# Attention rows in runs of 40, a new order of loads and weight turns between forward and GLU, and du placed ahead on VectorE

## The chip, the cores and the metric

The kernel runs on one core of one Trainium2 chip, as one launch. The metric is device time in microseconds (us); the kernel before has a median of 3124.64 us in three runs. The engines are called PE (TensorE, the matmuls), DVE (VectorE), ACT (ScalarE), POOL (GpSimd) and SP (SyncE, which here only issues DMAs); POOL and ACT issue DMAs too.

## The reference

The kernel computes a block with attention over segments and a gated linear unit (GLU), and the gradients of all eleven differentiable inputs. Cut to the forward function, for S = 2048 rows, D = 512, 32 heads of 128, F = 1792:

```python
mod = silu(c) @ w_mod                      # six rows: sa, ca, ga, sb, cb, gb
h = layernorm(x) * (1 + ca) + sa
# attention, segment after segment: 8 memory rows + 32 rows of h
for s in range(64):
    hs = concat([mem, h[32*s:32*s+32]])    # 40 rows
    q, k, v = hs @ Wq, hs @ Wk, hs @ Wv    # 32 heads
    o = softmax(mask(q @ k.T * scale)) @ v
    o = o @ Wo
    mem, a[32*s:32*s+32] = o[:8], o[8:]
x = x + ga * a
h = layernorm(x) * (1 + cb) + sb
out = x + gb * ((sigmoid(h @ w_gate) * (h @ w_up)) @ w_down)
# and the vector-Jacobian product of all this with grad_out
```

The memory rows of a segment come from the segment before, so forward attention is one chain of 64 steps.

## The kernel before, in words

Inputs, weights and most tiles are bf16, sums are f32 in PSUM. There are three stages, one after the other:

- Forward attention (to about 1000 us): a loop over the 64 segments. Four weights, Wq, Wk, Wv and Wo, lie in SBUF. Each segment's probabilities, values and outputs are stored to DRAM for the backward pass (PS, VT, OT, OSR: 352 KB each). Of a segment's 40 output rows, the 8 memory rows are needed at once and the rest only in the GLU. The 8 memory rows and the first 24 of the others are worked out and stored at once (32 rows of AOA, `store_rows` after `tail.split()`); the last 8 rows of four segments are worked out together as a "tail" (`TailRows`) and stored as 32 rows of AOB. Names in PE's records: `ao_tps` are the tail's products, `ao_b_tp` its last turn.
- GLU, forward and backward together (1000 to about 1380 us): 16 tiles of 128 rows go through a software pipeline of seven steps, s0 to s6, in iterations; within one iteration the deepest step (the oldest tile) comes first. w_gate, w_up, w_down lie over the SBUF of Wv and Wk, their turned copies w_gateT and w_upT over Wq.
- Then the weight gradients of the GLU (w_down's chunks, `gps`/`mm` at L1164), and backward attention, of some 1700 us, which the change doesn't touch but for its setup (`WoT`, L1313).

The steps of the GLU, with the names that the records show:

- s0 (L985): `t0` = attention rows x ga, `x1` = t0 + x0, statistics (`st`, `mv`, `ve` on DVE, `rstd` and `db` = dout x gb on POOL), `xhf`, `h2a`, `h2` on DVE. In the records t0 is `t`, x1 is `x`, h2 is `h`.
- s1 (L1021): two transposing DMAs on SP, `hdT<-h` and `hdT<-db`.
- s2 (L1027): four chunks of 448 columns; gate matmuls (L1039), sigmoid on ACT to `sg`, up matmuls (L1043), copy on ACT to `u`; then `hh` = sg x u on DVE, and `umh` = u - hh on POOL.
- s3: `dp` matmuls (hdT of db by w_downT); `du` = dp x sg on DVE in four pieces (L1064), reading PSUM and so freeing the PSUM buffers which later matmuls need; `dg` = du x umh on DVE (L1065).
- s4: `b` = hh by w_down (14 matmuls); transposing DMAs duT and dgT; `b_bf` on ACT; then t1 = b x gb on DVE (L1084, `t`), `o_sb` = t1 + x1 on POOL (L1086) with the store of the output, and `pr_gb` = dout x b on DVE (L1089).
- s5: the gradient of h (28 matmuls); `dh2b` on ACT, `dxh`, `pr_cb`, `junk`, `ta`, `dx` on DVE, `tb` on ACT; `da` = dx x ga on DVE (L1127), `pr_ga` = dx x attention rows on POOL (L1130).
- s6: column sums on PE (`acc_ps`), the turn of da and its store (DAOT).

PSUM has five buffers for the matmuls (psM) and two for the turns (psT).

What sets the order: a scheduler may move instructions of an engine at build time, except where the code pins what is traced between two points (`self.pin`, `pin_behind`). In the kernel before, SP and PE are not among the engines pinned at the end of the GLU, and their order at the seam is the scheduler's: SP issues dout of the first tiles and all the loads of attention rows before the transposing DMAs. The DMAs of one queue use eight completion semaphores in turn, on SP and on POOL, so that each issue waits until the DMA of eight issues before has landed. POOL issues its DMAs (stores, and the GLU's weights at L810) in line with its arithmetic.

At the seam, before: the last segment issues the modulation rows (`mod_bc`, four loads of one row, broadcast over the partitions, into `bcs[2..5]`) and the loads of tile 0 on SP; on POOL the weights in the order w_down, w_up, w_gate; then the late K and Q rows of the last segment (`late_rows`); the turns of the last probabilities (ET, L725) and values (Vst), the end of the tail, and `bcs[4]` + 1. The turns of w_down (L969) come with s0 of tile 0, those of w_up and w_gate (L958) with s0 of tiles 1 and 2; because PE's order is the scheduler's, all those of w_down and w_up were placed before tile 0's first matmul, and evacuated by DVE and ACT in turn.

The loads of attention rows of a tile before are eight DMAs, in `load_x_rows`:

```python
for s4 in range(4):
    q.dma_start(dst[s4 * T:s4 * T + 24, :], a[4 * j + s4, M:32, :])
    q.dma_start(dst[s4 * T + 24:(s4 + 1) * T, :], b[j, 8 * s4:8 * s4 + 8, :])
```

At the end of the GLU, `accs` (a tile of the pool) takes acc_ps and goes to DMOD by four DMAs on POOL; its pool memory is reused by the stage after.

Of the kernel before, what the change touches and what calls it, by code (L numbers as in the profile page):

```python
# [40 lines left out]
class K:  # L41
# [43 lines left out]
    def alloc_dram(self):  # L85
# [6 lines left out]
        self.AOA = d("AOA", [NS + 1, 32, cfg.D], BF16)  # L92
        self.AOB = d("AOB", [NS // 4, 32, cfg.D], BF16)
# [231 lines left out]
    def store_rows(self, psp, pool, ft, dram, name, tag, then=None):  # L325

        nc = self.nc
        tb = pool.tile([128, 128], BF16, name=name + "_tb", bufs=1 if name.endswith("_b") else 2)
        nc.vector.tensor_copy(tb[:].rearrange("p (r c) -> p c r", c=self.cfg.DC), ft[:])

        def f():
            tp = psp.tile([128, 128], BF16, name=name + "_tp", tag=tag)
            nc.tensor.transpose(tp[:], tb[:], self.ident[:])
            rb = pool.tile([128, 128], BF16, name=name + "_rb")
            nc.vector.tensor_copy(rb[:], tp[:])
            nc.gpsimd.dma_start(dram.rearrange("r (c x) -> (r c) x", x=128), rb[:])
            if then is not None:
                then(rb)

        self.later.append(f)  # L340
# [91 lines left out]
    def phase2(self):  # L432
# [13 lines left out]
        with ExitStack() as ctx:  # L446
# [201 lines left out]
            tail = TailRows(self, sb2, psp, psp, 1, "ao", self.AOB, 2, ptag="p")  # L648
# [24 lines left out]
            for s in range(NS):  # L673
# [119 lines left out]
                if s == NS - 1:  # L793
                    for i in range(2, 6):
                        self.mod_bc(None, i, "", t=self.bcs[i])
                    self.glu_first = self.glu_load(0, nc.sync)
# [12 lines left out]
                else:  # L809
                    nc.gpsimd.dma_start(self.w_down, io["B_w_down"].rearrange("(fc p) d -> p fc d", p=128))  # L810
                    nc.gpsimd.dma_start(self.w_up, io["B_w_up"].rearrange("(c p) f -> p c f", p=128))
                    nc.gpsimd.dma_start(self.w_gate, io["B_w_gate"].rearrange("(c p) f -> p c f", p=128))
                    late_rows()
# [56 lines left out]
                self.store_rows(psp, sb2, ft, self.AOA[s + 1], "at", "p")  # L870
# [9 lines left out]
                if s < NS - 1:  # L880
                    norms.append(norm)
            for pi in range(NP):
# [9 lines left out]
            tail.finish()  # L892
# [19 lines left out]
    def glu_load(self, j, q):  # L912
        io, D = self.io, self.cfg.D
        r0, r1 = j * 128, (j + 1) * 128
        x0, a_rows, dout = self.ring_x0[j % 2], self.ring_a[j % 6], self.ring_dout[j % 7]
        q.dma_start(dout, io["grad_out"].rearrange("o s d -> (o s) d")[r0:r1, :])
        self.load_x_rows(a_rows, j, self.AOA[1:], self.AOB, q)
        q.dma_start(x0, io["A_x"].rearrange("o s d -> (o s) d")[r0:r1, :])
        return dict(x0=x0, a_rows=a_rows, dout=dout)

    def phase3(self):
# [9 lines left out]
        with ExitStack() as ctx:  # L931
# [19 lines left out]
            def wT_piece(src, dst, fc0, n, k):  # L951
                def f():
                    for fc in range(fc0, fc0 + n, 2):
# [6 lines left out]
                        self.evac("act" if (fc // 2 + k) % 2 else "dve", dst[:, fc:fc + m, :],  # L960
# [3 lines left out]
            def wdT_piece(c):  # L964
                def f():
                    for f0 in range(0, FC, 7):
# [7 lines left out]
            pieces = {0: [wdT_piece(c) for c in range(DC)],  # L974
                      1: [wT_piece(w_up, w_upT, 0, 8, 0), wT_piece(w_up, w_upT, 8, 6, 0)],
                      2: [wT_piece(w_gate, w_gateT, 0, 8, 1), wT_piece(w_gate, w_gateT, 8, 6, 1)]}
# [3 lines left out]
            def load(j):  # L980
                if j >= NT or j in ins:
                    return
                ins[j] = self.glu_first if j == 0 else self.glu_load(j, nc.sync)

            def s0(j):  # L985
                r0, r1 = j * 128, (j + 1) * 128
                load(j + 1)
                for f in pieces.pop(j, []):
                    f()
# [60 lines left out]

            def s3(j, st):
# [6 lines left out]
                for ch in range(NCH):  # L1058
# [5 lines left out]
                    nc.vector.tensor_tensor(du[:, sl], dp[:, 0:CH], sg[:, sl], op=ALU.mult)  # L1064
                nc.vector.tensor_tensor(dg[:], du[:], umh[:], op=ALU.mult)  # L1065
# [5 lines left out]
            def s4(j, st):  # L1071
# [11 lines left out]
                t1 = sbp.tile([128, D], F32, name="t1", tag="f32tmp", bufs=5)  # L1083
                nc.vector.tensor_tensor(t1[:], b_bf[:], gb_bc[:], op=ALU.mult)  # L1084
                o_sb = sbp.tile([128, D], BF16, name="o_sb", bufs=2)
                nc.gpsimd.tensor_tensor(o_sb[:], t1[:], st["x1"][:], op=ALU.add)  # L1086
                nc.gpsimd.dma_start(out_rows[r0:r1, :], o_sb[:])
                pr = sbp.tile([128, D], BF16, name="pr_gb", bufs=3)
                nc.vector.tensor_tensor(pr[:], st["dout"][:], b_bf[:], op=ALU.mult)  # L1089
                st.update(duT=duT, dgT=dgT, pr=pr)  # L1090
                return st

            def s5(j, st):
# [7 lines left out]
                xh2, rstd, dout, a_rows = st["xh2"], st["rstd"], st["dout"], st["a_rows"]  # L1101
                dh2b = sbp.tile([128, D], BF16, name="dh2b", bufs=1)
# [24 lines left out]
                nc.vector.tensor_tensor(da[:], dx1[:], ga_bc[:], op=ALU.mult)  # L1127
                nc.gpsimd.dma_start(self.DAROWS[r0:r1, :], da[:])
                pr3 = sbp.tile([128, D], BF16, name="pr_ga", bufs=1)
                nc.gpsimd.tensor_tensor(pr3[:], dx1[:], a_rows[:], op=ALU.mult)  # L1130
                st.update(dh2b=dh2b, pr2=pr2, pr3=pr3, da=da)
# [38 lines left out]
            def after(it):  # L1170
                if it == NT + 1:
# [7 lines left out]

            self.run_pipeline(NT, [s0, s1, s2, s3, s4, s5, s6], deepest_first=True, after=after)  # L1180
            ET = mybir.EngineType
            self.pin_behind(i0, self.pinned, [ET.DVE, ET.Activation, ET.Pool])
            accs = sbp.tile([128, D], F32, name="accs", bufs=1)
# [758 lines left out]
class TailRows:  # L1942
# [45 lines left out]
    def split(self):  # L1988
# [5 lines left out]
        def summed():  # L1994
            ft = self.k.fold_sum(self.psp, parts, self.name + "_b", "p")
            self.k.store_rows(self.psp, self.pool, ft, self.dram_b[s0 // 4], self.name + "_b", "p")
# [96 lines left out]
```

The softmax here doesn't subtract the row's maximum and nothing guards it: scores larger than these inputs give would overflow.

## Time and profile before

| quantity | us |
|---|---|
| median of three runs | 3124.64 (3122.74 to 3125.85) |
| the profiled execution | 3127.18 |
| its span | 3125.4 |
| last attention product of forward on PE | 996.1 |
| first gate matmul of tile 0 | 1036.43 |
| start of the second tile's third step and on: steady tiles | 1083 to 1302 |
| last column sums of the GLU | 1379.5 |

The profiled execution is 1.78 us longer than its span: the span runs from the first to the last record of an engine. "Busy" of an engine is the time in which one of its instructions runs. A line of the timeline gives start, duration, engine, line of the code, operation with output and inputs, and, in brackets, the idle time of that engine just before and what ended it. The granted clock of PE is given as a share of full speed. Means by stage, in the GLU's steady tiles: PE 18.91 us busy of 20.13 or 19.70, DVE 15.56 or 15.13, POOL 12.17 or 12.30, ACT 7.25.

### The profile page before, as it was taken

The page shows a single profiled execution, that of the slowest core. Times are in us where ns is not written, and L with a number is a line of the kernel's source. Part 1 is how long each engine was busy: PE and PEld are TensorE (multiplying, and loading weights), DVE is VectorE, ACT ScalarE, POOL GpSimd, SP SyncE. Part 2 cuts the span into 40 slices and gives each one's busy share as a digit, 9 for nine tenths or more (in the row PEclk, how much of TensorE's full clock was granted, in tenths as well). Part 3 has the DMA queues.
Part 4 walks back from the last instruction along what each step waited for, and adds up shares of the span by engine and source line. Part 5 has one row for each costly group of instructions (what it writes and reads, how often), then busy time and mean ns, then how long its engine had stood idle before and what let it go on. Part 6 is the DMA issues. An engine that isn't in the chain of part 4 may idle for free.

```text
span 3125.4 us, 106126 instructions
## 1 busy us (share of the span) xinstructions
PE 3004.2 (96%) x43769; PEld 1838.1 (59%) x43845; DVE 1616.2 (52%) x3738; ACT 1264.6 (40%) x3053; POOL 1473.0 (47%) x2974
## 2 busy tenths in 40 slices
PE   5999999999998799989989999999999999999999
PEld 3666666666665444445567777777777754455454
DVE  4556656655654777733255555555655542322321
ACT  2555555555554433322155555555555530110111
POOL 3666666666665466531144444444444432233322
PEclk8999999999999899999999999999999999999999
DMA  8887788788787798898589999999999998666674
GB/s 295 214 214 199 205 214 212 204 207 213 205 207 237 177 214 219 202 267 271 185 218 244 240 248 242 244 243 248 244 239 244 243 270 285 201 202 213 196 234 147
DMA packets 844665, 703.54 MB, mean 225 GB/s; under 512 B 543794, under 2 KB 716370, under 8 KB 843796
## 3 DMA queue, kind: packets, MB, share of 16 engines
q1 hardware_dynamic: 714404, 486.69, 62.2%
q0 software_dynamic: 59120, 148.64, 14.6%
q10 hardware_dynamic: 70656, 61.41, 6.3%
q8 instruction: 345, 5.65, 0.8%
q14 instruction: 140, 1.15, 0.1%
HBM read 294.93 MB, written 276.35 MB: 183 GB/s over the span
## 4 chain that ended last, share of the span: by engine, by line
PE 50%; issue 4%; DMA 2%; POOL 1%; DVE 0%; SPq 0%; ACT 0%; POOLq 0%; DVEq 0%
PE gps L1885 10%; PE dh_ps L216 8%; PE g_ps L1547 6%; PE pass_ps L256 5%; PE gps5o L1899 4%; PE dhq_ps L224 4%; PE gps L1234 3%; PE dh_tps L216 3%; PE dp_ps L1526 2%; PE tps L1459 2%; PE dp_ps L1534 1%; PE turn_ps L1413 1%; PE dh_ft L321 1%; PE gps L1164 1%; PE wtp L1300 1%
## 5 line engine op out<-in xcount | busy, mean ns | idle before, releaser
L1885 PE MATMUL gps<-rows,hrows 128*128 128x512 bf16 (+2 forms) x2124 | 415.6, 355 | 1.9
L1885 PEld LDWEIGHTS <-hrows 128*128 128x128 bf16 x2160 | 211.2, 98 | 204.6
L256 PEld LDWEIGHTS <-hT 128*32 128x32 bf16 x6144 | 158.2, 97 | 161.3 <-issue 1.9
L1591 POOL COPY dOst<-RAd 96x512 bf16<-96x512 bf16 x128 | 75.4, 613 | 311.3 <-DVE RAd L63 311.1
L1889 POOL DMA_DIRECT2D out_dram<-ot x108 | 81.4, 754 | 258.6 <-DVE ot L63 132.3
L63 DVE CAST ot<-gps 128x512 bf16<-128x512 f32 (+3 forms) x76 | 48.1, 633 | 284.9 <-PE gps L1885 191.6
L875 POOL TENSOR_TENSOR Pst<-Pst,rden 120x1408 bf16<-120x1408 bf16 x63 | 159.6, 2533 | 57.4 <-issue 38.9
L61 ACT ACTIVATE ot<-gps 128x512 bf16<-128x512 f32 (+3 forms) x75 | 41.3, 551 | 356.2 <-PE gps L1885 225.3
L61 ACT ACTIVATE dVT<-g_ps 128x512 bf16<-128x512 f32 (+1 forms) x192 | 109.3, 569 | 95.9 <-PE g_ps L1547 95.5
L63 DVE CAST RA0v<-pass_ps 128x512 bf16<-128x512 f32 x128 | 88.5, 692 | 89.5 <-PE pass_ps L256 86.2
L216 PE MATMUL dh_ps<-WvT,dVT 128*32 128x512 bf16 x2048 | 133.4, 380 | 0.0
L256 PE MATMUL pass_ps<-Wv,hT 128*32 128x512 bf16 x2048 | 133.3, 380 | 0.0
L1899 PE MATMUL gps5o<-WoT,rows 128*128 128x512 bf16 x580 | 127.8, 379 | 1.0 <-DMA rows<-OSR 0.3
L224 PE MATMUL at_ps<-Wo,OT 128*32 128x256 bf16 x4096 | 125.0, 275 | 0.1
L256 PE MATMUL pass_ps<-Wk,hT 128*32 128x512 bf16 x2048 | 123.3, 383 | 1.5 <-ACT hT L865 1.1
L1536 DVE SCALAR_TENSOR_TENSOR dS<-dp_ps,Pst_l 128x512 bf16<-128x512 f32 (+1 forms) x192 | 112.0, 639 | 22.8 <-PE dp_ps L1534 22.8
L256 PE MATMUL pass_ps<-WoT,dyT 128*32 128x256 bf16 (+1 forms) x3072 | 122.4, 308 | 0.9 <-ACT dyT L1665 0.9
L224 PE MATMUL dhq_ps<-WqT,dQT 128*32 128x256 bf16 x4096 | 122.9, 273 | 0.0
L216 PE MATMUL dh_ps<-WkT,dKT 128*32 128x512 bf16 x2048 | 122.3, 380 | 0.0
L256 PE MATMUL pass_ps<-Wq,hT 128*32 128x512 bf16 x2048 | 121.6, 379 | 0.0
L224 PEld LDWEIGHTS <-dQT 128*32 128x32 bf16 x4096 | 109.6, 97 | 15.9
L709 ACT ACTIVATE ET<-st_ps 128x480 bf16<-128x480 f32 (+1 forms) x192 | 96.1, 535 | 42.6 <-ACT qT L61 34.7
(419 smaller groups left out, 7164.5 us busy)
## 6 DMA issues: line engine op xcount, KB each, us to landing
OSR<-Ost SPq DMA_DIRECT2D x64, 352.0 KB
OT<-OT SPq DMA_DIRECT2D x64, 352.0 KB
VT<-VTr SPq DMA_DIRECT2D x64, 352.0 KB
PS<-Pst SPq DMA_DIRECT2D x64, 352.0 KB
OT_l<-OT SPq DMA_DIRECT2D x64, 352.0 KB
Pst_l<-PS SPq DMA_DIRECT2D x64, 352.0 KB
VT_l<-VT SPq DMA_DIRECT2D x64, 352.0 KB
DVR<-rows_x POOLq DMA_DIRECT2D x64, 352.0 KB, 6.4
```

The costliest lines, as they stand in the source:

```text
L61: return nc.scalar.activation(out, in_, AF.Copy)
L63: return nc.vector.tensor_copy(out, in_)
L216: self.nc.tensor.matmul(ps[32 * j:32 * j + 32, :], lhsT=lhsT, rhs=w, start=(n < 4), stop=(n >= total - 4), tile_position=(0, 32 * j))
L224: nc.tensor.matmul(ps[32 * j:32 * j + 32, :], lhsT=x[k], rhs=w[k][:, 256 * d:256 * d + 256], start=(n == 0), stop=(n == total - 1), tile_p ...
L256: self.nc.tensor.matmul(ps[32 * j:32 * j + 32, :], lhsT=lhs(c), rhs=rhs, start=(c == 0), stop=(c == DC - 1), tile_position=(0, 32 * j))
L709: nc.scalar.activation(part3(ET, pi)[:, 0:n, 0:120], st_ps[:, 0:n, 0:120], AF.Exp, scale=cfg.scale)
L875: nc.gpsimd.tensor_tensor(Pst[0:120, :, :], Pst[0:120, :, :], rden[:, :].unsqueeze(2).to_broadcast([120, G, 128]), op=ALU.mult)
L1234: nc.tensor.matmul(ps[:], lhsT=h2r[:, j, c * 128:(c + 1) * 128], rhs=xr[:, j, :], start=(j == 0), stop=(j == NT - 1))
L1536: nc.vector.scalar_tensor_tensor(out=part3(dS, pi), in0=ps[:, 0:n, :], scalar=cfg.scale, in1=part3(Pst, pi), op0=ALU.mult, op1=ALU.mult)
L1547: nc.tensor.matmul(ps[:, j, :], lhsT=lh[:, g * GW:(g + 1) * GW], rhs=rh[:, g * GW:(g + 1) * GW], start=True, stop=True)
L1885: nc.tensor.matmul(ps[:, 0:ng * E], lhsT=hrows[:, tp_, c * 128:(c + 1) * 128], rhs=rows[:, tp_, 0:ng * E], start=(tp_ == 0), stop=(tp_ == ...
L1899: nc.tensor.matmul(pss[gg][:], lhsT=src[0][:, src[1], gg * E:(gg + 1) * E], rhs=dyrows[:, tp_, :], start=(tp_ == order[0]), stop=(tp_ == o ...
```

## The change

- AOA gets 40 rows for each segment: the 8 memory rows, the first 24 of the others, and behind them the 8 of the tail, so that a segment's 32 rows lie together. The tail's 8 rows of each of four segments are stored by four DMAs on POOL instead of one (64 instead of 16 in all), and a tile's attention rows are loaded by four DMAs of 32 rows instead of eight. A tile's loads come in the order x0, attention rows, dout.
- In the last segment `late_rows` and tile 0's loads are issued first, then the modulation rows in the order 2, 4, 3, 5; the weights are loaded in the order gate, up, down; tile 1's loads and the end of the tail come before the last turns of ET and Vst.
- w_gate is turned first, ahead of the pipeline, and evacuated by ACT alone; w_down is turned after iteration 2, w_up after iterations 3 and 4. PE and ACT are pinned up to iteration 2, and at the end of the GLU PE and SP are pinned too.
- In each iteration, what makes the output of b (t1, o_sb and its store) and what makes da (da and its store) is put in a list `late`, which s3 empties after its du (and the end of the iteration, if s3 didn't). pr_gb moves from s4 to s5 of the next iteration, with two buffers instead of three. On DVE the order of a steady tile becomes dx, two du, da, two du, t (of b), dg, t (of s0), pr_gb, x, and so on as before; before it is dx, t (of b), da, pr_gb, four du, t, dg, x. POOL's order becomes DX1ROWS, pr_ga, DAROWS, DUROWS, o_sb, DGROWS, output; before it is DX1ROWS, pr_ga, DAROWS, o_sb, output, DUROWS, DGROWS.
- accs is laid into the region of Wk behind w_gate and w_up instead of the pool.

The number and size of the matmuls and transposes stay as they are.

```diff
@@ -91,4 +91,3 @@
         self.H1ROWS = d("H1ROWS", [cfg.S, cfg.D], BF16)
-        self.AOA = d("AOA", [NS + 1, 32, cfg.D], BF16)
-        self.AOB = d("AOB", [NS // 4, 32, cfg.D], BF16)
+        self.AOA = d("AOA", [NS + 1, cfg.M + cfg.T, cfg.D], BF16)
         self.VT = d("VT", GL, BF16)
@@ -335,3 +334,6 @@
             nc.vector.tensor_copy(rb[:], tp[:])
-            nc.gpsimd.dma_start(dram.rearrange("r (c x) -> (r c) x", x=128), rb[:])
+            if callable(dram):
+                dram(rb)
+            else:
+                nc.gpsimd.dma_start(dram.rearrange("r (c x) -> (r c) x", x=128), rb[:])
             if then is not None:
@@ -647,3 +649,9 @@
             mod_at = sorted([4 * i + 4 for i in range(4 * DC - 1)] + [7])
-            tail = TailRows(self, sb2, psp, psp, 1, "ao", self.AOB, 2, ptag="p")
+            def rows_b(rb, b):
+
+                for i in range(4):
+                    nc.gpsimd.dma_start(self.AOA[4 * b + i + 1, 32:32 + M, :].rearrange("r (c x) -> (r c) x", x=128),
+                                        rb[32 * i:32 * i + 32, :])
+
+            tail = TailRows(self, sb2, psp, psp, 1, "ao", rows_b, 2, ptag="p")
 
@@ -793,5 +801,6 @@
                 if s == NS - 1:
-                    for i in range(2, 6):
+                    late_rows()
+                    self.glu_first = {0: self.glu_load(0, nc.sync)}
+                    for i in (2, 4, 3, 5):
                         self.mod_bc(None, i, "", t=self.bcs[i])
-                    self.glu_first = self.glu_load(0, nc.sync)
                 st_exp(0)
@@ -809,6 +818,5 @@
                 else:
-                    nc.gpsimd.dma_start(self.w_down, io["B_w_down"].rearrange("(fc p) d -> p fc d", p=128))
-                    nc.gpsimd.dma_start(self.w_up, io["B_w_up"].rearrange("(c p) f -> p c f", p=128))
                     nc.gpsimd.dma_start(self.w_gate, io["B_w_gate"].rearrange("(c p) f -> p c f", p=128))
-                    late_rows()
+                    nc.gpsimd.dma_start(self.w_up, io["B_w_up"].rearrange("(c p) f -> p c f", p=128))
+                    nc.gpsimd.dma_start(self.w_down, io["B_w_down"].rearrange("(fc p) d -> p fc d", p=128))
                 den(1, or2)
@@ -869,3 +877,3 @@
                 tail.split()
-                self.store_rows(psp, sb2, ft, self.AOA[s + 1], "at", "p")
+                self.store_rows(psp, sb2, ft, self.AOA[s + 1, 0:32, :], "at", "p")
                 if s4 == nseg_t - 1:
@@ -881,2 +889,4 @@
                     norms.append(norm)
+            self.glu_first[1] = self.glu_load(1, nc.sync)
+            tail.finish()
             for pi in range(NP):
@@ -891,3 +901,2 @@
             nc.sync.dma_start(self.VT[NS - 1], VTr[:])
-            tail.finish()
             nc.vector.tensor_scalar_add(self.bcs[4], self.bcs[4], 1.0)
@@ -915,5 +924,6 @@
         x0, a_rows, dout = self.ring_x0[j % 2], self.ring_a[j % 6], self.ring_dout[j % 7]
-        q.dma_start(dout, io["grad_out"].rearrange("o s d -> (o s) d")[r0:r1, :])
-        self.load_x_rows(a_rows, j, self.AOA[1:], self.AOB, q)
         q.dma_start(x0, io["A_x"].rearrange("o s d -> (o s) d")[r0:r1, :])
+        for i in range(4):
+            q.dma_start(a_rows[32 * i:32 * i + 32, :], self.AOA[4 * j + i + 1, self.cfg.M:self.cfg.M + self.cfg.T, :])
+        q.dma_start(dout, io["grad_out"].rearrange("o s d -> (o s) d")[r0:r1, :])
         return dict(x0=x0, a_rows=a_rows, dout=dout)
@@ -959,3 +969,3 @@
                                                     self.ident[:])
-                        self.evac("act" if (fc // 2 + k) % 2 else "dve", dst[:, fc:fc + m, :],
+                        self.evac("act" if k is None or (fc // 2 + k) % 2 else "dve", dst[:, fc:fc + m, :],
                                   tp[:, 0:m * DC, :].rearrange("p (i c) d -> p i (c d)", i=m))
@@ -973,5 +983,4 @@
 
-            pieces = {0: [wdT_piece(c) for c in range(DC)],
-                      1: [wT_piece(w_up, w_upT, 0, 8, 0), wT_piece(w_up, w_upT, 8, 6, 0)],
-                      2: [wT_piece(w_gate, w_gateT, 0, 8, 1), wT_piece(w_gate, w_gateT, 8, 6, 1)]}
+            turns = {2: [wdT_piece(c) for c in range(DC)],
+                     3: [wT_piece(w_up, w_upT, 0, 8, 0)], 4: [wT_piece(w_up, w_upT, 8, 6, 0)]}
 
@@ -982,3 +991,3 @@
                     return
-                ins[j] = self.glu_first if j == 0 else self.glu_load(j, nc.sync)
+                ins[j] = self.glu_first.get(j) or self.glu_load(j, nc.sync)
 
@@ -987,4 +996,2 @@
                 load(j + 1)
-                for f in pieces.pop(j, []):
-                    f()
                 st = ins.pop(j)
@@ -1050,2 +1057,8 @@
 
+            late = []
+
+            def flush():
+                while late:
+                    late.pop(0)()
+
             def s3(j, st):
@@ -1064,2 +1077,3 @@
                     nc.vector.tensor_tensor(du[:, sl], dp[:, 0:CH], sg[:, sl], op=ALU.mult)
+                flush()
                 nc.vector.tensor_tensor(dg[:], du[:], umh[:], op=ALU.mult)
@@ -1082,10 +1096,12 @@
                 nc.scalar.activation(b_bf[:], bp[:], AF.Copy)
-                t1 = sbp.tile([128, D], F32, name="t1", tag="f32tmp", bufs=5)
-                nc.vector.tensor_tensor(t1[:], b_bf[:], gb_bc[:], op=ALU.mult)
-                o_sb = sbp.tile([128, D], BF16, name="o_sb", bufs=2)
-                nc.gpsimd.tensor_tensor(o_sb[:], t1[:], st["x1"][:], op=ALU.add)
-                nc.gpsimd.dma_start(out_rows[r0:r1, :], o_sb[:])
-                pr = sbp.tile([128, D], BF16, name="pr_gb", bufs=3)
-                nc.vector.tensor_tensor(pr[:], st["dout"][:], b_bf[:], op=ALU.mult)
-                st.update(duT=duT, dgT=dgT, pr=pr)
+
+                def out():
+                    t1 = sbp.tile([128, D], F32, name="t1", tag="f32tmp", bufs=5)
+                    nc.vector.tensor_tensor(t1[:], b_bf[:], gb_bc[:], op=ALU.mult)
+                    o_sb = sbp.tile([128, D], BF16, name="o_sb", bufs=2)
+                    nc.gpsimd.tensor_tensor(o_sb[:], t1[:], st["x1"][:], op=ALU.add)
+                    nc.gpsimd.dma_start(out_rows[r0:r1, :], o_sb[:])
+
+                late.append(out)
+                st.update(duT=duT, dgT=dgT, b_bf=b_bf)
                 return st
@@ -1101,2 +1117,4 @@
                 xh2, rstd, dout, a_rows = st["xh2"], st["rstd"], st["dout"], st["a_rows"]
+                pr = sbp.tile([128, D], BF16, name="pr_gb", bufs=2)
+                nc.vector.tensor_tensor(pr[:], dout[:], st["b_bf"][:], op=ALU.mult)
                 dh2b = sbp.tile([128, D], BF16, name="dh2b", bufs=1)
@@ -1126,7 +1144,11 @@
                 da = sbp.tile([128, D], BF16, name="da", bufs=2)
-                nc.vector.tensor_tensor(da[:], dx1[:], ga_bc[:], op=ALU.mult)
-                nc.gpsimd.dma_start(self.DAROWS[r0:r1, :], da[:])
+
+                def out():
+                    nc.vector.tensor_tensor(da[:], dx1[:], ga_bc[:], op=ALU.mult)
+                    nc.gpsimd.dma_start(self.DAROWS[r0:r1, :], da[:])
+
+                late.append(out)
                 pr3 = sbp.tile([128, D], BF16, name="pr_ga", bufs=1)
                 nc.gpsimd.tensor_tensor(pr3[:], dx1[:], a_rows[:], op=ALU.mult)
-                st.update(dh2b=dh2b, pr2=pr2, pr3=pr3, da=da)
+                st.update(dh2b=dh2b, pr2=pr2, pr3=pr3, da=da, pr=pr)
                 return st
@@ -1170,2 +1192,6 @@
             def after(it):
+                for f in turns.pop(it, []):
+                    f()
+                if it == 2:
+                    self.pin(i0, [ET.PE, ET.Activation])
                 if it == NT + 1:
@@ -1179,6 +1205,13 @@
 
-            self.run_pipeline(NT, [s0, s1, s2, s3, s4, s5, s6], deepest_first=True, after=after)
             ET = mybir.EngineType
-            self.pin_behind(i0, self.pinned, [ET.DVE, ET.Activation, ET.Pool])
-            accs = sbp.tile([128, D], F32, name="accs", bufs=1)
+            wT_piece(w_gate, w_gateT, 0, FC, None)()
+            later = after
+
+            def after(it):
+                flush()
+                later(it)
+
+            self.run_pipeline(NT, [s0, s1, s2, s3, s4, s5, s6], deepest_first=True, after=after)
+            self.pin_behind(i0, self.pinned, [ET.PE, ET.DVE, ET.Activation, ET.Pool, ET.SP])
+            accs = self.flat(self.Wk, 2 * DC * F, 2 * D, F32)
             nc.vector.tensor_copy(accs[:], acc_ps[:, :])
@@ -1995,3 +2028,5 @@
             ft = self.k.fold_sum(self.psp, parts, self.name + "_b", "p")
-            self.k.store_rows(self.psp, self.pool, ft, self.dram_b[s0 // 4], self.name + "_b", "p")
+            to = self.dram_b
+            to = (lambda rb: self.dram_b(rb, s0 // 4)) if callable(to) else to[s0 // 4]
+            self.k.store_rows(self.psp, self.pool, ft, to, self.name + "_b", "p")
 
```

## The prediction

> **What bounds the kernel now.** I read the page first: busy shares and slices.
>
> ```profile
> span 3125.4 us, 106126 instructions
> PE 3004.2 (96%) x43769; PEld 1838.1 (59%) x43845; DVE 1616.2 (52%) x3738; ACT 1264.6 (40%) x3053; POOL 1473.0 (47%) x2974
> PE   5999999999998799989989999999999999999999
> PEclk8999999999999899999999999999999999999999
> ```
>
> TensorE (PE) is busy 96% of the span; the change keeps all its matmuls and transposes, so only PE's idle time and cold clock can be won. A slice is 78 us; PE dips at the start and in the slices around 1015 to 1094 us, where forward ends and the GLU starts. Next, PE's waits from 995 to 1400 us (columns: who waited for what, us in total, times, longest):
>
> ```profile
> PE mm L1043 <- DVE du L1064: 16.3, 15, 3.4
> PE mm L1039 <- DMA hdT<-h: 10.1, 1, 10.1
> PE tp L969 <- DMA Wv<-in_B_w_down_dram: 6.4, 1, 6.4
> PE wtp L1313 <- DVE WoT L63: 4.3, 1, 4.3
> ```
>
> The last three are single holes; the first recurs in every tile. Third, PE's timeline of the seam (start, duration, operation, count, in brackets the idle before):
>
> ```profile
> 997.09 0.79 PE L725 MATMUL tps<-ident,ET 128*128 128x128 bf16 x11
> 1004.30 1.46 PE L969 MATMUL tp<-ident,Wv 128*128 128x128 bf16 x12 [6.43 <-DMA Wv<-in_B_w_down_dram]
> ...
> 1036.43 1.68 PE L1039 MATMUL mm<-Wk,hdT 128*128 128x448 bf16 x4 [10.08 <-DMA hdT<-h]
> ...
> 1040.38 0.92 PE L1043 MATMUL mm<-Wk,hdT 128*128 128x448 bf16 x4
> ```
>
> From 1000 to 1040 us PE is busy only 12.30 + 7.12 us of 40, at a granted clock of 0.74; the first groups of tile 0 take 1.68 us where 0.92 is warm. What holds tile 0 is the transposing DMA of h, late on SP though h was ready on VectorE (DVE) at 1024.65:
>
> ```profile
> 1031.07 1.21 SPq L1024 DMA_TRANSPOSE hdT<-db  x1
> ...
> 1033.98 1.19 SPq L1023 DMA_TRANSPOSE hdT<-h  x1
> ```
>
> SP is busy there with loads of attention rows, eight per tile, each 0.29 to 0.54 us. Last, one steady tile on DVE, GpSimd (POOL) and PE:
>
> ```profile
> 1145.84 2.07 DVE L1127 TENSOR_TENSOR da<-dx,Wv 128x512 bf16<-128x512 f32 x1
> 1147.83 0.41 DVE L1089 TENSOR_TENSOR pr_gb<-Wk,b_bf 128x512 bf16<-128x512 bf16 x1
> 1148.17 2.20 DVE L1064 TENSOR_TENSOR du<-mm,sg 128x448 bf16<-128x448 f32 x4
> ```
> ```profile
> 1146.18 1.17 POOL L1130 TENSOR_TENSOR pr_ga<-dx,Wv 128x512 bf16<-128x512 f32 x1
> ...
> 1148.79 1.28 POOL L1086 TENSOR_TENSOR o_sb<-t,x 128x512 bf16<-128x512 f32 x1
> ```
> ```profile
> 1148.83 0.92 PE L1043 MATMUL mm<-Wk,hdT 128*128 128x448 bf16 x4 [1.16 <-DVE du L1064]
> ```
>
> da should take about 0.7 us and takes 2.07: it stands until pr_ga on POOL has ended (1147.35) and is done 0.56 us after that; PE waits 1.16 us for the du behind it. This wait is 1.17 us in six tiles (period 20.13) and 0.74 in the next five (19.70).
>
> **What the Trainium skill says.** "SBUF — State Buffer", "Who interferes with whom": a VectorE operation with two SBUF inputs and a GpSimd operation that reads SBUF exclude each other, each blocking the other to its end; one SBUF input and one from PSUM does not contend. The trace agrees: x (two SBUF inputs) took 3.35 us at 1047.67 beside umh, pr_gb 5.31 us at 1061.58 beside umh and o_sb, but du (PSUM input) 0.55 us apiece beside o_sb. "TensorE: Matmul & The Clock Gate", Part 1 "The HAM clock gate": an idle TensorE drops to half clock and needs some busy microseconds to come back; the 0.74 and the 1.68 against 0.92 above agree. "DMA: Bandwidth & Descriptors", "Queues, rings and completion order": DMAs don't complete in order of issue. The program gives each DMA queue eight completion semaphores in turn, so an SP issue waits for the landing of the one eight before; the trace shows this at 996.80 to 1011.71, where SP's issues stand 2.5 to 3.9 us apart.
>
> **The change part by part.** The sum is made against the profiled run, 3127.18 us (1.8 outside the span), and carried over to the median, 2.54 below it.
>
> 1. Start of tile 0. Call S the start of its first gate matmul, 1036.43 before. In the new order SP issues the last segment's K and Q rows, x0, four row loads and dout of tile 0, and then the four modulation rows (landed 999.25, 1003.15, 1005.7 and 1009 before; 1003 to 1010 expected). DVE does its Pst work until about 1006.2, then t0 to h, 6.9 us in the steady tile (1150.30 to 1157.2): h at 1012.5 to 1013.5. SP comes free of the modulation rows' semaphores at 1009 to 1012, and has about 17 issues of 0.4 us (loads of tiles 1 and 2, stores) and hdT<-db (1.25) ahead of hdT<-h: issued near 1020, and with 1.19 us of issue and 1.25 to land S = 1022 (1017 to 1028). The turns of w_gate (56 transposes, all evacuated by ACT) lie ahead of that, in time that was idle; this needs the gate weights first on POOL's queue, as the change has it. Gain 14.4.
>
> 2. Given back within the first tiles. The turns of w_down and w_up, before mostly done in idle time, now stand between iterations 2 and 4: before, from S to the second s3 it took 46.9 us (to 1083.33); stage by stage (s2 of tile 0 7.7, w_down's turns with its first dp 9.1 bound by evacuation, s2 of tile 1 6.05, up turns and the rest) I get 49.2: loss 2.3. One more stall like the 3.39 us at 1067.47, half hidden: 1.5 (0 to 4). Seam in sum: −10.6 (−5 to −17).
>
> 3. Steady tile, iterations 6 to 16. Call D the end of dx (1145.24 in the tile shown). Two du (0.55 each) are done at D + 1.1, so the PE wait for the first du goes. But da is still blocked by pr_ga and ends at D + 2.6; then du 3 and 4 to 3.7, t to 4.3, dg to 5.4. By then o_sb (it needs t, and waits on POOL for the store DUROWS until 4.6) is pending; in the trace a pending POOL operation comes before the next DVE one (pr_ga, then pr_gb at 1147.83), so it runs from 5.4 to 6.5, t0 is blocked until 7.0, and pr_gb ends at 7.3. From x to the end of umh it is 10.77 us in both modes of before: D + 18.1. From there to the next D 2.36 (junk starts at umh's end, 1162.88, and then as from 1142.75): the cycle is 20.45 us. Before, the same count gives 19.87 and 19.44, under the PE-set 20.13 and 19.70. So DVE and POOL become the bound, and PE (18.95 us of work) waits 1.5 us a tile, now at the up matmuls. Over ten tiles and a first wait of 0.8: 15.8 against 12.25 after 1083 us before: loss 3.5. Bounds: if either da or t0 wins against POOL, the period is 19.4 to 19.55 and the part gains 7 to 8; with both 18.95, and 11 to 12; if x or dg also loses once to POOL (1.2 each, from pr_ga's duration), it loses 15.
>
> 4. Tail. accs lie elsewhere now, so DVE's first WoT evacuation waits only for the DAOT store, 3.1 us earlier (1385.0 for 1388.1); but the load of the next HHROWS piece now waits for the four DMOD stores and holds ACT's first WoT evacuation behind it on ACT's queue. PE's 4.34 us there shrinks by about 1; the last sums on PE stand two matmuls earlier: 0.43. Together −1.5 (−3 to +1).
>
> 5. Forward. The memory rows are stored by four DMAs for one, 3 x 0.55 us more on POOL in every fourth segment, 14 times in the loop. POOL is idle 3.19 us after such a group (912.63 to 915.82) and DVE's operations there read PSUM, so I take 0; bounds −3 to 14 x 1.65 = +23 if all of it reached PE.
>
> Sum: −10.6 + 3.5 − 1.5 = −8.6; 3127.18 becomes 3118.6, and the median 3124.64 becomes 3116.
>
> **The rivals.**
> A. As worked out: 3116 (own range 3108 to 3124).
> B. The du wait goes for good: DVE wins da or t0 (arbitration when both engines come free together isn't decided by what I see), and the tile is bound by PE. Part 3 turns from +3.5 to −7 or −11: 3124.64 − 10.6 − 8.5 − 1.5 = 3104. For it: PE's own work is 18.95; against: all three locked pairs seen went POOL's way.
> C. Slower: SP's eight semaphores. The 352 KB stores OSR, OT, PS and VT and the modulation rows are now ahead of hdT<-h and share the memory with 5.5 MB of weights (323 GB/s in 1000 to 1020 us). A landing as late as 1015 holds the issue eight later, and three such laps of 7 us put S at 1036 to 1040. With S = 1038 the seam costs 1.6 + 2.3 + 1.5 = 5.4; with +3.5 − 1.5 it is 3132. It decides from S = 1030.6 on, where parts 1 to 4 cancel. For it: the issues 2.5 to 3.9 us apart; against: the weights land by 1015 and there are 64 loads fewer in all.
> D. The change does less than it says: du stands only half ahead of da, and the extra stores of part 5 come through for half a microsecond in each of 16 groups (8 us): 3124.
>
> **How the numbers follow.** Chances: A 0.45, B 0.25, C 0.20, D 0.10. A measurement of this kernel can tell 0.2% (6.2 us) from no change, that is below 3118.4 or above 3130.9. A gives 0.31 faster, 0.13 same, 0.01 slower; B 0.25 faster; C 0.06 same and 0.14 slower; D 0.01, 0.08 and 0.01. In sum 0.57, 0.27, 0.16. The range 3100 to 3131 leaves out half of C and the best of B.
>
> **What would show it.** Part 1: hdT<-h issued near 1020, first gate matmul near 1022, clock of 1000 to 1040 above 0.74. Part 2: second s3 about 49 us after S. Part 3: no PE wait for the first du, a wait of about 1.5 us at an up group instead, period 20.45, da and t0 long on DVE; a period below 19.7 would show B. Part 4: the 4.34 us down to some 3. Part 5: equal time from the start to the last segment. A gate matmul after 1031, or a forward longer by over 3 us, makes the forecast wrong.

## The result and the profile after

The changed kernel takes 3121.30 us (median of four runs, 3119.25 to 3122.78) against 3125.24 us before (median of four, 3122.74 to 3126.91): a ratio of 0.9988 with an interval of 0.997 to 1.0005. That is 3.9 us less, and within what this measurement can tell from no change. The profiled execution took 3121.63 us, its span 3119.8.

The page's busy line and slices, PE's clock among them, as they were shown of before:

```profile
span 3119.8 us, 106172 instructions
PE 3005.8 (96%) x43845; PEld 1837.6 (59%) x43845; DVE 1644.2 (53%) x3735; ACT 1266.7 (41%) x3056; POOL 1502.8 (48%) x3022
PE   6999999999998899989989999999999999999999
PEclk8999999999999899999999999999999999999999
```

PE's dip in the slice after 1015 us is smaller (8 for 7), and DVE is busy 28.0 us longer, with three operations fewer (3735 for 3738). That is the first sign of what happened: in this profile an operation that stands still behind another engine counts as busy. PE's waits from 985 to 1400 us (who waited for what, us in total, times, longest):

```profile
PE mm L1046 <- DMA hdT<-h: 15.0, 1, 15.0
PE mm L1050 <- DVE du L1077: 10.3, 11, 0.9
PE mm L1186 <- DMA Wk<-HHROWS: 4.9, 1, 4.9
PE mm L1046 <- ACT b_bf L1096: 4.7, 10, 1.7
PE wtp L1346 <- DVE WoT L63: 2.3, 1, 2.3
```

The wait for w_down at the seam is gone; that for hdT is longer (15.0 for 10.1), but it begins and ends earlier. A wait for du is still there in eleven tiles, now in the second group of up matmuls and no longer in the first. Beside it stands one that the kernel before did not have: for b_bf on ACT, ten times. PE's and SP's timelines of the seam:

```profile
1008.30 0.61 PE L968 MATMUL tp<-ident,Wk 128*128 128x128 bf16 x8 [0.20 <-ACT Wq L61]
1023.93 1.67 PE L1046 MATMUL mm<-Wk,hdT 128*128 128x448 bf16 x4 [15.02 <-DMA hdT<-h]
```
```profile
1017.49 0.89 SPq L927 DMA_DIRECT2D Wv<-AOA  x2
1018.49 1.20 SPq L1031 DMA_TRANSPOSE hdT<-db  x1
1019.74 0.57 SPq L928 DMA_DIRECT2D Wk<-in_grad_out_dram  x1
1020.35 0.89 SPq L927 DMA_DIRECT2D Wv<-AOA  x2
1021.34 1.23 SPq L1030 DMA_TRANSPOSE hdT<-h  x1
```

The first gate matmul of tile 0 starts 12.5 us earlier (1036.43 before). hdT<-h is issued at 1021.34 for 1033.98, still behind loads of later tiles, though h was done at 1017.04. One steady tile, on DVE, on POOL and in part on PE (start, duration):

```profile
1213.54 2.81 DVE L1130 SCALAR_TENSOR_TENSOR junk<-dxh,xh 128x512 f32<-128x512 f32 x1
...
1217.54 0.69 DVE L1142 TENSOR_TENSOR dx<-ta,tb 128x512 f32<-128x512 f32 x1 [0.28 <-ACT tb L1140]
1218.15 1.15 DVE L1077 TENSOR_TENSOR du<-mm,sg 128x448 bf16<-128x448 f32 x2
1219.21 1.63 DVE L1147 TENSOR_TENSOR da<-dx,Wv 128x512 bf16<-128x512 f32 x1
...
1223.43 1.75 DVE L1000 TENSOR_TENSOR t<-Wv 128x512 f32<-128x512 bf16 x1
...
1237.97 0.69 DVE L1142 TENSOR_TENSOR dx<-ta,tb 128x512 f32<-128x512 f32 x1 [0.28 <-ACT tb L1140]
```
```profile
1212.20 3.58 POOL L1054 TENSOR_TENSOR umh<-u,hh 128x1792 bf16<-128x1792 bf16 x1
...
1219.12 1.17 POOL L1152 TENSOR_TENSOR pr_ga<-dx,Wv 128x512 bf16<-128x512 f32 x1
...
1222.77 1.87 POOL L1102 TENSOR_TENSOR o_sb<-t,x 128x512 bf16<-128x512 f32 x1
```
```profile
1218.04 0.92 PE L1046 MATMUL mm<-Wk,hdT 128*128 128x448 bf16 x4 [0.34 <-ACT b_bf L1096]
...
1221.43 0.92 PE L1050 MATMUL mm<-Wk,hdT 128*128 128x448 bf16 x4 [0.94 <-DVE du L1077]
```

From dx to dx, the period of a tile, it is 20.42 us (20.43 here). junk, which took 0.68 in the kernel before, stands until umh ends (1215.78) and takes 2.81; da stands behind pr_ga, t behind o_sb. tb on ACT needs what follows junk (bb and cc), and b_bf is behind tb on ACT (tb from 1216.70, b_bf from 1217.42): that is PE's new wait. The du that PE waits for is the third, which stands behind da.

The two profiled executions, cut at the same three events (at_ps is the last segment's own product; the 996.1 of the table before is a product of the tail, `ao_tps`):

| stretch | before | after | change |
|---|---|---|---|
| start to the last attention product (at_ps) | 992.97 | 991.20 | −1.8 |
| from there to dx of the first steady tile | 91.27 | 82.07 | −9.2 |
| from there to the last column sums | 294.91 | 300.83 | +5.9 |
| from there to the end of the span | 1746.25 | 1745.70 | −0.6 |

The first row is not shown to be an effect of the change: eight other kernels with its forward, run below, have 991.6 to 993.4 there, and two with the old forward 990.5 and 991.3.

### The profile page after: what moved, and what is told of

It reads as the page before. It is cut to its first block, busy times and chain, and to the rows that moved or that the text cites. A ratio compares the mean times of both kernels' runs of the same rounds, so it can differ in the third digit from the quotient of the medians.

```text
span 3119.8 us, 106172 instructions
## 1 busy us (share of the span) xinstructions
PE 3005.8 (96%) x43845; PEld 1837.6 (59%) x43845; DVE 1644.2 (53%) x3735; ACT 1266.7 (41%) x3056; POOL 1502.8 (48%) x3022
## 4 chain that ended last, share of the span: by engine, by line
PE 50%; issue 3%; DMA 3%; POOL 1%; DVE 0%; SPq 0%; ACT 0%; POOLq 0%; ACTq 0%; DVEq 0%
PE gps L1918 9%; PE dh_ps L215 8%; PE g_ps L1580 6%; PE pass_ps L255 5%; PE gps5o L1932 4%; PE dhq_ps L223 4%; PE gps L1267 3%; PE dh_tps L215 3%; PE dp_ps L1559 2%; PE tps L1492 2%; PE dp_ps L1567 1%; PE turn_ps L1446 1%; PE dh_ft L320 1%; POOL out_dram L1922 1%; PE wtp L1333 1%
## 5 line engine op out<-in xcount | busy, mean ns | idle before, releaser
L1624 POOL COPY dOst<-RAd 96x512 bf16<-96x512 bf16 x128 | 75.6, 612 | 312.7 <-DVE RAd L63 312.2
```

## The experiments

The theory after the result: the seam gains about 11 us, and the new order of the tile gives back 6 of them, as DVE and GpSimd now close a cycle longer than PE's (a cycle is a ring of operations, each behind the one before it, that comes back to its start one tile later; the longest sets the period). The rivals: the longer tile comes from the seam's parts; or du ahead is good, and something else lost. All ratios are to the kernel before, with 95% intervals; the change itself has 0.9988.

**The seam without the new tile order.** In s3, s4, s5 the lists are undone, and pr_gb goes back to s4 (the main lines):

```diff
-                flush()
                 nc.vector.tensor_tensor(dg[:], du[:], umh[:], op=ALU.mult)
...
-                late.append(out)
+                out()
```

> The changed kernel with the tile's old order of t, o_sb, da and pr_gb (all parts of the seam and the tail stay). Theory (the seam gains about 11 us, and the new tile order gives back 6 of it through the exclusion of VectorE and GpSimd): steady period back to 20.1 or 19.7, PE waits for the first du again (about 1.17 or 0.74 us a tile), total 3115 to 3116, some 9 us below before. Rival (the longer period comes from the seam's other parts, such as the SP order or the pin on PE): period stays at 20.42 and the total near 3121.

Measured: 3115.23 us, 0.9968 [0.9956, 0.9979]. The periods are 20.15 us and later 19.7, as before the change. The rival falls: the seam's parts alone are 9 us faster than the kernel before, and the tile order takes 6 of that. The ratios' intervals overlap a little, but the runs don't (3113.0 to 3117.9 here, 3119.3 to 3122.8 of the change), and in the traces the steady tiles take 220.4 us from first dx to last, for 226.0 in the changed kernel.

**The new tile order on the kernel before.** The opposite half: `late`, `flush` and pr_gb in s5, all else old.

> The kernel before with the new order of the tile alone. Theory: steady period 20.42, no PE wait for the first du but one of about 0.9 us at the second up group and a short one for b_bf, total 6 us above before: 3131. Rival (du ahead pays, and what the steady tile lost came from elsewhere): period 19.0 to 19.6, total 3115 to 3120.

Measured: 3127.77 us, 1.0014 [1.0008, 1.0021], slower than before, by 3 to 4 us and not 6. The period is 20.40. The seam of this kernel is 2.4 us shorter than before by the events of the table (88.84 for 91.27), which accounts for most of the difference; why the new order helps there wasn't looked into. The ratios of the two halves multiplied give 0.9982, within the interval of the change.

**umh on VectorE, on the changed kernel and on the one before.**

```diff
-                nc.gpsimd.tensor_tensor(umh[:], u[:], hh[:], op=ALU.subtract)
+                nc.vector.tensor_tensor(umh[:], u[:], hh[:], op=ALU.subtract)
```

> The changed kernel with umh = u - hh on VectorE instead of GpSimd (about 1.08 us there as for hh, instead of 3.58). Theory (the cycle through umh and the operations that it excludes sets the period): junk falls from 2.81 to 0.68 us, the cycle falls under PE's 18.95, period 18.9 to 19.2, so about 1.3 us in each of eleven tiles: total 3105 to 3108. Rival (VectorE's own work or ACT's order sets the period, so that one more operation on VectorE makes it longer): period 20.4 to 21.5, total 3121 or more.

> The kernel before with umh on VectorE. Theory: period 20.13 and 19.70 fall too, as VectorE comes free before du is wanted; PE's wait for du goes or stays at da's block by pr_ga (at most 0.7): period 18.9 to 19.5, total 3113 to 3118. Rival: period unchanged or longer, total 3125 or more.

On the changed kernel: 3102.00 us, 0.9922 [0.991, 0.9935]. Its DVE timeline (two dx, with umh and junk between them):

```profile
1148.46 0.69 DVE L1142 TENSOR_TENSOR dx<-ta,tb 128x512 f32<-128x512 f32 x1 [0.28 <-ACT tb L1140]
...
1162.68 1.09 DVE L1054 TENSOR_TENSOR umh<-u,hh 128x1792 bf16<-128x1792 bf16 x1
...
1165.38 0.68 DVE L1130 SCALAR_TENSOR_TENSOR junk<-dxh,xh 128x512 f32<-128x512 f32 x1
...
1167.26 0.69 DVE L1142 TENSOR_TENSOR dx<-ta,tb 128x512 f32<-128x512 f32 x1 [0.28 <-ACT tb L1140]
```

and its row of the windows from 1100 to 1300 us (length, busy time of PE, PEld, DVE, ACT and POOL, clock, DMA share, GB/s):

```profile
1100.00:1300.00 200.00, 199.42 (x1033) 95.98 (x1042) 177.94 (x281) 75.77 (x136) 91.72 (x123) 1.00 1.01 227
```

The period is 18.80, junk takes 0.68, and PE is busy 199.4 of 200 us, without a single wait. One operation more on VectorE makes the tile shorter: what cost was the exclusion, not VectorE's work. da and t (1.59 and 1.75) are still held behind pr_ga and o_sb there, and cost nothing now.

On the kernel before: 3116.38 us, 0.9972 [0.9962, 0.9982]. The time is as the theory said, and its reason is wrong: the period stays at 20.12 and 19.70, and the wait for du as well (11.8 us in 13 tiles). The gain lies in the first tiles (from the last attention product to the first steady dx 85.0 us for 91.3) and the last (from the last steady dx to the last column sums 73.0 for 75.6); the profiled execution itself took 3122.75, as its part behind the GLU, which the edit doesn't touch, was 6.6 us longer than in that of before. So in the old order another cycle closes the tile, one without umh. The next run tests that.

**The old tile order with the seam of the change and umh on VectorE** (the first edit and the third together).

> The seam of the changed kernel with the tile's old order, and umh on VectorE. Theory (two cycles: in the old order PE, dx, da and the first du close one of 20.13 or 19.70 us without umh in it; in the new order umh closes one of 20.42): period stays at 20.1 or 19.7, and the total near 3112 to 3115. Rival (umh was the cost in both orders, and du ahead adds nothing): period 18.8 and total 3102.

Measured: 3111.16 us, 0.9953 [0.994, 0.9965]; the period is 20.13 and 19.70. Its tile on PE and DVE shows the other cycle:

```profile
1158.08 0.92 PE L1050 MATMUL mm<-Wk,hdT 128*128 128x448 bf16 x4 [1.15 <-DVE du L1077]
...
1167.05 3.19 PE L1116 MATMUL mm<-Wq,dgT 128*128 128x512 bf16 x14
```
```profile
1170.90 0.69 DVE L1123 SCALAR_TENSOR_TENSOR dxh<-mm,Wv 128x512 f32<-128x512 f32 x1 [2.31 <-ACT dh2b L1120]
...
1174.00 0.69 DVE L1141 TENSOR_TENSOR dx<-ta,tb 128x512 f32<-128x512 f32 x1 [0.28 <-ACT tb L1139]
1174.61 0.69 DVE L1099 TENSOR_TENSOR t<-b_bf,Wv 128x512 f32<-128x512 bf16 x1
1175.21 2.06 DVE L1146 TENSOR_TENSOR da<-dx,Wv 128x512 bf16<-128x512 f32 x1
```

From the up matmuls at 1158.08 PE needs 12 us to the end of the products with dgT; then dh2b, dxh to dx, t, da (held by pr_ga) and pr_gb go before the first du, 7.9 us more; then PE may go on, at 1178.19, 20.1 us after it last did. VectorE is idle 2.31 us in front of dxh. Making VectorE or GpSimd free elsewhere doesn't touch this cycle; putting du ahead of da cuts it, and then the cycle through umh is next. The four corners, all on the change's seam:

| order on DVE | umh on GpSimd | umh on VectorE |
|---|---|---|
| old | 3115.2 (20.15, 19.7) | 3111.2 (20.13, 19.70) |
| du ahead | 3121.3 (20.42) | 3102.0 (18.80) |

(in brackets the period). du ahead costs 6 us in one column and gains 9 in the other.

**What holds tile 0 at the seam.** First SP's order; the loads of tiles 2 and later stay behind the transposing DMAs of tile 0:

```diff
-                    self.pin(i0, [ET.PE, ET.Activation])
+                    self.first = self.pin(i0, [ET.PE, ET.Activation, ET.SP]), len(self.traced())
...
+            self.pin_behind(self.first[1], self.first[0], [ET.SP])
```

> The changed kernel with SP also pinned in program order up to iteration 2, so that the two transposing DMAs of tile 0 stand directly behind the stores PS and VT, and the loads of tiles 2 and later behind them. Theory (S is held by the loads that SP issues ahead of hdT<-h): hdT<-h issued as soon as h is ready, near 1017.1, first gate matmul near 1019.6 instead of 1023.9, total 4 us lower: 3117. Rival (h itself or the landing is late for another reason, such as the memory's share): first gate matmul within 1 us of 1023.9, total 3121.

Measured: 3118.80 us, 0.9975 [0.9966, 0.9984], 2.5 us under the changed kernel by the medians and 0.0013 by the ratios (4 us), with intervals that overlap. hdT<-h is issued within 0.1 us of h; from the last attention product to the first gate matmul it is 29.85 us for 32.73. But dx of the first steady tile comes only 0.8 us earlier (81.24 for 82.07): of the 2.9 us won at the first matmul 0.6 is lost again by the end of w_down's turns, and 1.5 in the matmuls of the next tile, where PE now waits 1.17 us for a du.

Then POOL, where the last group's four stores wait for the weights' completion semaphores ahead of tile 0's rstd (changed kernel, idle before in brackets):

```profile
1004.57 0.50 POOL L653 DMA_DIRECT2D AOA<-ao_b_rb  x1 [2.45 <-DMA Wk<-in_B_w_up_dram]
1011.47 1.47 POOL L653 DMA_DIRECT2D AOA<-ao_b_rb  x3 [6.41 <-DMA Wv<-in_B_w_down_dram]
...
1013.13 0.57 POOL L1011 TENSOR_TENSOR rstd<-ve,mhalf 128x1 f32<-128x1 f32 x1
```

VectorE had ve ready at 1009.8. Two edits; the last group's stores on ACT's queue:

```diff
-                    nc.gpsimd.dma_start(self.AOA[4 * b + i + 1, 32:32 + M, :].rearrange("r (c x) -> (r c) x", x=128),
+                    (nc.scalar if b == NS // 4 - 1 else nc.gpsimd).dma_start(self.AOA[4 * b + i + 1, 32:32 + M, :].rearrange("r (c x) -> (r c) x", x=128),
```

> The changed kernel with the last four stores of the tail's rows on ACT's queue instead of POOL's. On POOL they stood from 1001.7 to 1011.5 waiting for the completion semaphores of the weight loads, with the rstd of tile 0 behind them. Theory: rstd starts near 1010 and h is ready near 1013.5 instead of 1017.0, but SP's order still holds hdT<-h at 1021: first gate matmul at 1023.9, total 3121 (at most 1 us lower). Rival (POOL's wait sets S): first gate matmul near 1020, total 3117.

Measured: 3127.40 us, 1.0005 [0.9997, 1.0013], 6 us over the changed kernel, which neither reading expected. ACT's timeline:

```profile
1014.26 1.98 ACTq L653 DMA_DIRECT2D AOA<-ao_b_rb  x4
1016.34 1.47 ACT L61 ACTIVATE VTr<-tps 128x512 bf16<-128x512 bf16 x3 [16.16 <-DMA AOA<-ao_b_rb]
```

In this program ACT's DMAs take turns with SP's at the same eight completion semaphores, so that the stores on ACT waited for SP's last stores of OSR and OT (352 KB each) and two of its loads of tile 1, and the evacuations of VTr and w_gate's turns stood behind them: the wait moved to an engine that had more behind it. The same edit, SP's order and umh on VectorE together:

> umh on VectorE, SP pinned and the four stores on ACT's queue, all three on the changed kernel. Theory: period 18.8 as with umh on VectorE alone, and first gate matmul near 1016.5 (h near 1013.5, SP free of VT's issue at 1013.7): total 7 us under that of umh alone: 3095. Rival: the two parts of the seam don't add up, since the weights or the rows of the tiles behind come late: 3098 to 3102.

Measured: 3102.40 us, 0.9929 [0.9916, 0.9941], nothing gained on umh alone, for the same reason (PE waits 13.9 us for an evacuation of w_gate on ACT). The other edit keeps the stores on POOL and makes one of four:

```diff
-                for i in range(4):
-                    nc.gpsimd.dma_start(self.AOA[4 * b + i + 1, 32:32 + M, :].rearrange("r (c x) -> (r c) x", x=128),
-                                        rb[32 * i:32 * i + 32, :])
+                nc.gpsimd.dma_start(self.AOA[4 * b + 1:4 * b + 5, 32:32 + M, :].rearrange("i r (c x) -> i (r c) x", x=128),
+                                    rb[:])
```

> The changed kernel with one DMA for the tail's rows of four segments instead of four, everything else the same. Theory: the forward doesn't move (the extra issues on POOL were hidden): last segment's attention product within 1 us of 991.2 to 992.2; rstd comes near 1010.5, but SP's order still holds hdT<-h: first gate matmul at 1023 to 1024, total 3120 to 3121. Rivals: the forward was longer by the stores and comes down by some 8 us: 3113; or POOL's wait set the first matmul: near 1020, total 3117.

> umh on VectorE, SP pinned, and the tail's rows of four segments stored by one DMA on POOL instead of four (so no store waits for a weight load's semaphore ahead of rstd). Theory: rstd near 1010.5, h near 1013.5, hdT<-h issued near 1014.5 behind VT, first gate matmul near 1018 (1023.9 in the changed kernel, 1022.0 with SP pinned alone), period 18.8, total 3095 to 3096. Rival: landing of hdT or of the rows shares memory with the weights until 1012 to 1015, so nothing comes below umh alone plus the pinned SP: 3099 or more.

Alone it gives 3121.63 us, 0.9985 [0.9978, 0.9993]: the forward doesn't move (last attention product at 993.03), so the 48 extra stores were hidden. rstd does start earlier, 19.3 us after the last attention product for 21.9, but h is done 26.2 us after it for 25.8, and the first gate matmul starts 33.3 us after it for 32.7: POOL's wait alone doesn't hold tile 0. With SP's order and umh on VectorE: 3101.31 us, 0.9917 [0.9905, 0.9929], the fastest of all, but not separable from umh alone. rstd starts at 1010.39 as expected, yet h is done only at 1017.4. VectorE's line for it:

```profile
1016.67 0.69 DVE L1022 TENSOR_TENSOR h<-h2a,Wv 128x512 bf16<-128x512 f32 x1 [1.40 <-DMA VT<-VTr]
```

The buffer of h lies where VTr of the forward lay, and waits until VTr's store has landed. It is the same in the changed kernel, where POOL's late rstd hides it:

```profile
1013.32 0.32 SPq L901 DMA_DIRECT2D VT<-VTr  x1
```
```profile
1016.36 0.68 DVE L1023 TENSOR_TENSOR h<-h2a,Wv 128x512 bf16<-128x512 f32 x1
```

h starts 3.0 us after the issue of VTr's store there, 3.1 with this edit and 3.2 with the one store alone, and SP issues that store only behind its waits for semaphores. So two waits end close together in front of h, and taking out POOL's alone gains nothing. It wasn't tried with another place for h.

**The order of the weights.** The changed kernel with w_down, w_up, w_gate as before the change (three lines swapped).

> The changed kernel with the weights loaded in the old order w_down, w_up, w_gate, everything else the same; w_gate now lands last. Theory (S is held by h and SP's order, the turns of w_gate only have to be done by then): the turns start near 1012 and end near 1021 with their evacuations, first gate matmul at 1023 to 1025, warm sooner, total 3120 to 3122. Rival (the weights' order carries the seam's gain): the turns start after 1015, first gate matmul near 1027 or later, total 3124 or more.

Measured: 3123.07 us, 0.9991 [0.9983, 1.0]. The turns of w_gate run from 1010.7 to 1017.7 and tile 0 starts at 1025.33, 1.0 us later after the last attention product than in the changed kernel. The total is 1 us above what was expected and 1 us below the rival's. The new order of the weights carries little of the seam's gain.

**accs in the pool again.**

```diff
-            accs = self.flat(self.Wk, 2 * DC * F, 2 * D, F32)
+            accs = sbp.tile([128, D], F32, name="accs", bufs=1)
```

> The changed kernel with accs back in the pool. Theory: the tail's gain of 1.2 us is lost, PE's wait for WoT's evacuation goes from 2.3 to about 4.3 us, total 3122 to 3123. Rival (the tail's wait is set by the order of the last tiles, not by where accs lies): wait stays near 2.3, total 3121.

Measured: 3121.58 us, 0.9985 [0.9978, 0.9991]; PE's wait for WoT is 2.50 us. The rival holds: where accs lies changes nothing that can be seen. PE's wait there is 4.34 us before and 1.6 to 4.4 in the other kernels; what sets it wasn't settled. This kernel and the one with one store for four run like the change, and more often (21 and 16 runs): both have 0.9985 with an interval below 1. So the change's own gain, which its four runs don't separate from nothing, is likely real, at some 0.15%.

## Why the prediction came out as it did

The forecast was 3116 with a range of 3100 to 3131; measured were 3121.3. It forecast a gain beyond 0.2% as likeliest, and the measured gain is 0.12%. The range takes in the time of the kernel before, so that lying within it says little; the parts say more.

- Start of tile 0: S at 1023.93 for 1022 and hdT<-h issued at 1021.34 for 1020 look right, with luck in it: 1.8 us are the earlier end of the forward, which belongs to no part. Counted from the last attention product, S comes after 32.73 us for 43.46 before, a gain of 10.7 and not 14.4. The working had h ready at 1013 and SP late; h was at 1017.0. POOL's stores behind the weights and the landing of VTr's store both stood in front of it, and the step had neither on its list. The pinned SP shows that the issues ahead of hdT<-h did hold it, for about 3 us. The clock of 1000 to 1040 us, which was to rise above 0.74, was 0.70; PE stood still for 15.0 us in front of tile 0.
- Given back: from S to the first steady dx 49.34 us for 47.81, a loss of 1.5 for 3.8, which makes good most of what the start lacks. The seam in sum gained 9.2 for 10.6 (with the 1.8 us of the forward, which belong to no part, 11.0).
- Steady tile: the mechanism and the period are as forecast, 20.42 for 20.45 us. That the old order was bound by the cycle through PE and not by the one through umh is shown too, as moving umh left its period as it was. "The Trainium skill", page "SBUF — State Buffer", "Who interferes with whom", names the exclusion that it rests on; the trace agrees for da, t and junk, and moving umh took 1.6 us off the period. The loss was mis-sized: the sum took "ten tiles and a first wait of 0.8" and set two later waits of before (0.74 and 0.79) against it. By periods it is 11 tiles of 20.45 against 219.3 us, 5.6 and not 3.5. Measured from dx to dx, 226.0 us, 6.7 more, 1.3 of them in one tile of 21.75 us, in which POOL issued a store 2.9 us late and umh started late behind it; 0.7 comes back in the last tiles. PE's wait was forecast as 1.5 us at the up matmuls; it is 0.94 there and 0.34 at the gate matmuls, for b_bf behind tb on ACT.
- Tail: wrong in its reason. −1.5 was forecast from where accs lies; that edit alone is worth 0.3 us by medians, within its noise. Measured is −0.6, with the reason open.
- Forward: right, nothing, by the run with one store for four.

So the profiled execution, 3121.63 for 3118.6, is off by 2.4 us in the steady tile, counted by waits where the period should have been counted, by 1.4 at the seam and 0.9 in the tail, less the 1.8 of the forward, which lie within the spread of the other kernels. The medians are off by 5.3, as the forecast took 2.5 us off for the profiled execution of before, which lay that far above the median of three, while that of after lies 0.3 above its own. Rival B failed: in all eleven steady tiles da and t were held (1.62 and 1.75 us), so that VectorE never won against a GpSimd operation that was waiting. Of rival D, the 8 us for the extra stores weren't there (one store for four). The slower rival C (S at 1036 to 1040) failed: the semaphores did hold SP, from 1001.7 to 1011.4, but for one lap and not three.

## What to carry to other kernels

A wait that recurs in a loop closes a cycle, so before cutting it, add up the next longest cycle through the same engines: here it was 1 to 4% longer than the one that was cut, and the same edit lost 6 us with it and gained 9 without it. An operation that excludes others costs what stands behind it, so that umh was better for 1.09 us on the busier VectorE than for 3.58 us on GpSimd. In a program like this one a DMA waits at its issue for a completion semaphore that an older, larger DMA may hold, and what stands behind it on the issuing engine waits too; look at that before moving it to another queue.

## What was not expected of the hardware

PE kept its 199.4 us of 200 beside a VectorE at 89% (177.9 us, held operations included): the tile's period came down to 18.80 us, under the 18.95 that the forecast had taken for PE's own work from the kernel before. The difference goes with the number of PE's stops. The period less the waits shown is 18.80 us with no stop a tile, 18.96 with one (20.13 less 1.17, and 19.70 less 0.74, before) and 19.14 with two (20.42 less 0.94 and 0.34, after). From these an estimate: a stop costs PE 0.16 to 0.17 us more than the wait shown. No run tests it by itself.

And hdT<-h issued 1.3 us ahead of hdT<-db (SP pinned) let PE start 2.5 us after its issue had ended, but 1.4 us when it was issued last: with two transposing DMAs close together, the first did not land first by the margin of its issue. The other run with SP pinned that wasn't held elsewhere (the one with umh on VectorE and one store) shows the same 2.5 us; it was not tested by itself.
